# The keys of the last six chunks turned by DMA instead of on TensorE, and most of the instruction order rewritten

## The chip, the cores and the metric

The kernel runs on one core of a Trainium2 chip. The core has a matrix engine (TensorE, PE in the profile, with its weight loads listed as PEld), three engines for elementwise work (VectorE or DVE, ScalarE or ACT, GpSimd or POOL), a sequencer that issues transfers (SyncE or SP), and 16 DMA engines that carry them out. Every engine runs its own instructions strictly in the order in which they were written; engines wait for one another by semaphores. The metric is the device time of one execution in microseconds. Before the change its median over 13 runs was 153.55 us (152.85 to 154.96).

## The reference

The computation is a linear-attention layer followed by a feed-forward layer, on 4 sequences of 768 positions, with 8 heads of 48 channels (384 in all).

```python
for t in range(S):
    cur = np.einsum('bhd,bhe->bhde', u[None] * kt, vt)
    y[:, :, t] = np.einsum('bhd,bhde->bhe', rt, state + cur)
    state = w[None, :, :, None] * state + np.einsum('bhd,bhe->bhde', kt, vt)
...
xn = (x - mu) / np.sqrt(var + 1e-06) * g_ln
ch = np.maximum(xn @ w_ch1, 0.0) @ w_ch2
return x + ch
```

Here `r`, `k`, `v` are [4, 8, 768, 48], `x` is the attention output brought to [4, 768, 384], `w_ch1` is 384 × 1536 and `w_ch2` is 1536 × 384. All inputs and the output are float32; the kernel multiplies in bfloat16.

## The kernel before

The 768 positions of each sequence are cut into 6 chunks of 128 (`NCH`), so there are 24 chunks, numbered 0 to 23 (`NT`). In a chunk the recurrence becomes matrix products. A chunk i passes through these steps, whose names are the words of the written order:

- `k`, `v`, `r` load the inputs on SP's queue (L180, L186); one `r` serves two chunks. Buffers for k and v number 7 each (`LD`).
- `sck` scales the keys by powers of the decay into one of four bfloat16 buffers (L361, on DVE or POOL); `scr` does the same for r, in two halves (L364).
- `TK` turns the scaled keys on PE: four transposes of 128 × 128 into the PSUM bank `tr` (L379). `kT` copies the result to SBUF (L383, on ACT or DVE). `TR` and `rT` do this for r (L394, L400).
- `q` multiplies rT by the turned keys (L411). Chunks from 8 on (`QP`) take the keys straight from PSUM, as long as they are turned on PE (`qp(i)`). `cc` sums q with the bonus weights on PE (L438), `cp` copies that out (L449), `Vb` multiplies it into v (L453, POOL).
- `at` multiplies kT by rT on PE, giving the scores (L418); `A` masks them on DVE (L428).
- `kv` multiplies the keys by the values (L469); `S` adds the state (L484) and `Z` applies the decay (L493 or L497), giving the state for the next chunk. `vc` casts v (L370).
- `y` puts state and scores together on PE (L509, L521), `x` adds the bonus on DVE (L534), `xn` centres (L548, L552), `sq` and `rs` give the variance (L561, L572).
- `lc` turns xn into `xT`: for chunks from 8 on by a DMA transpose on SP (L613), before that on PE (`ln`).
- `up` multiplies by the first weights (L630), `re` is the rectifier (L644 on ACT, L646 on DVE), `dn` multiplies by the second weights (L657), `ot` adds x (L667), `st` stores (L678). `up` and `re` work on groups: chunks 0 to 5 alone, then pairs, so groups 6 to 14 hold chunks 6 and 7 up to 22 and 23; `up12_3` is unit 3 of group 12. `dn18` has three parts.

Which instruction follows which is given by `ORDER` (L23 to L67), a list of these words. A suffix names the engine (`.V` DVE, `.A` ACT, `.G` POOL, `.S` SP) where it differs from the default. `Planner.order` walks the list and emits each step; the costs and due times given to `add` (L762 on) play no part any more, but each step's needs are asserted to stand ahead of it. So the list fixes the sequence of every engine, and also of SP's queue of loads, stores and transposes. PE alternates between attention steps and the large products `up` and `dn`, which fill it up.

`KP` (L590) is the first chunk whose keys are turned by DMA; before the change it is 24, so none is. The branch for it is there (L785: a step `kT` on SP that calls `transpose_k_by_dma`, L385). The step `sckb` (L768) says what has to be done before a scaled-key buffer is written again.

Of the kernel before, what the change touches and what calls it, by code (L numbers as in the profile page):

```python
# [29 lines left out]
up2_2 re2_2.V rT5.A TK4 kT4.A q4.G kv3 Z3 up1_1 re1_1.V at4 A4 vc4.G xn3.A w2l1 ln3 up2_1 lc3.A cc4 cp4.A TK5 sq1  # L30
w2s03.V re2_1.A w2s02.G Vb4 up3_2 kv4 w2s01.V rs0 w2s11.G kT5.A w2s00.A y4 x4 xn4.A w2s13.A w2s10.A w2l2 up3_1
re3_1.A w2s20.G at5 dn00 r3 scr31.G q5.V re3_2.V w2s12.V ln4 lc4.V Z4 up3_0 re3_0.A dn01 cc5 v5 w2s23.A w2s22.A
cp5.A Vb5 A5 up4_2 up4_0 w2s21.V dn02 re4_2.A up4_1 scr30.V TR3 sq4 k6 ot0 sq2 sq3 vc5.V y5 r4 re4_1.V k7 rT7.A
rT6.A dn10 dn11 re4_0.A x5 xn5.V ln5 lc5.V dn12 ot1 sck6.G TK6 scr40.G sck7.V up5_0 up5_1 v6 rs1 kT6.A q6.V TK7
kT7.A scr41.V at6 A6 cc6 cp6.A Vb6 dn20 st0.S TR4 q7.V vc6.A kv6 Z6 re5_1.A k8 rT9.A rT8.A dn21 y6 x6 sck8.G at7
A7 dn22 ot2 xn6.A TK8 cc7 cp7.A v7 up5_2 re5_0.A kT8.A re5_2.A vc7.G kv7 S7 Vb7 k10 k9 sck9.G v8 y7 Z7.G x7 xn7.A
r5 dn30 q8 vc8.A at8 A8 v9 k12 dn31 st1.S r6 scr50.G ln6 lc6.V dn32 ot3 cc8 y8 ln7 sq5 lc7.A kv8 S8 dn40 cp8.A
TK9 kT9.A q9 up6_2 dn41 v10 k11 st2.S v12 v13 sq6 scr51.G up6_1 re6_1.A re6_2.A vc9.V sck10.V cc9 cp9.A TR5 Vb8
x8 dn42 rs2 k13 xn8.V lc8 Z8.G scr61.G ot4 Vb9 scr60.G at9 A9 up6_3 kv9 S9 Z9.G dn50 r7 rT11.A rT10.A TK10 q10
sck11.V re6_3.A kT10.A sq7 dn51 y9 x9 up6_4 re6_4.A sck12.V xn9.A lc9 rs3 vc10.G at10 TK11 cc10 q11 kT11.A cp10.A  # L40
up6_0 re6_0.A dn52 A10 up6_5 re6_5.A TR6 st4.A rT13.A rT12.A vc12.G y10 kv10 Vb10 ot5 dn60 at11 dn61 x10 S10
Z10.G cc11 cp11.A A11 xn10.V sck13.G scr70.G v11 vc11.V k15 TK12 kT12.A st5.A dn62 k14 k18 up7_4 at12 re7_4.A
Vb11 up7_5 q12 ot6 re7_5.A sq8 y11 cc12 cp12.A TK13 scr71.G lc10 r8 sq10 dn70 up7_0 up7_2 A12 kT13.V x11 q13
xn11.A lc11 re7_2.V TR7 y12 rT14.A rT15.A vc13.V at13 kv12 Z12 v14 A13 Vb12 up7_1 re7_1.A re7_0.A sq9 sck14.G
dn71 cc13 TK14 cp13.V kT14.V q14 dn72 kv13 up7_3 re7_3.A x12 ot7 xn12.A sck15.G S13 scr81.G scr80.G up8_4 TK15
kT15.V at14 k16 sq12 A14 dn80 up8_3 y13 rs4 re8_3.A sq11 re8_4.A q15 dn81 at15 k17 TR8 rT16.A r9 st3.S cc14
cp14.A up8_5 rT17.A re8_5.A dn82 up8_1 vc14.G Vb13 Z13.V x13 sck16.V TK16 Vb14 xn13.V A15 up8_0 kv14 v15 vc15.G
v17 lc12 st6.S re8_1.A up8_2 sck17.G ot8 dn90 q16 S14 Z14.V scr91.G sck18.G y14 x14 lc13 kT16.A re8_2.A sq13
scr90.V v16 k20 dn91 at16 cc15 dn92 re8_0.A cp15.V A16 ot9 Vb15 TK17 up9_3 kT17.A v23 st8.S v19 r10 k19 xn14.V
lc14 k21 vc17.G rs5 kv15 up9_1 re9_1.A y15 q17 S15 Z15.G vc16.A re9_3.A dn100 x15 xn15.V lc15 TR9 rT19.A at17  # L50
up9_2 cc16 dn101 v21 A17 re9_2.V cp16.V up9_0 re9_0.A dn102 rT18.V scr101.G Vb16 rs6 kv16 up9_4 ot10 S16 Z16.G
TK18 kT18.A sck19.V dn110 y16 x16 st9.S re9_4.A v18 scr100.G dn111 up9_5 cc17 q18 v22 re9_5.A dn112 at18 sq14 A18
TK19 cp17.A kT19.A up10_5 re10_5.A up10_0 y17 vc18.G r11 Vb17 cc18 cp18.A up10_1 vc19.G ot11 st11.A Vb18 q19
sck20.G st10.S k23 TR10 dn120 re10_0.V up10_4 xn16.V rT21.V lc16 dn121 scr111.G sck21.G vc21.A kv18 dn122 x17 Z18
ot12 st12.S rT20.A re10_1.A at19 A19 TK20 kT20.A cc19 y18 dn130 up10_3 at20 cp19.A re10_4.A xn17.A lc17 q20 TK21
kT21.A x18 dn131 A20 up10_2 q21 re10_2.V dn132 ot13 sq18 scr110.G re10_3.A TR11 rT23.V sq15 Vb19 rs7 sq16 kv19
S19 k22 sck22.V v20 y19 x19 rT22.A dn140 up11_1 sq17 re11_1.A dn141 cc20 st13.A cp20.A TK22 kT22.A dn142 at21
up11_0 up11_4 xn18.A vc22.V sck23.V q22 TK23 ot14 xn19.V lc18 lc19 st14.S A21 Z19.G rs8 vc20.G kv20 Vb20 S20
Z20.G re11_0.A kT23.A y20 up11_5 dn150 re11_4.V at23 x20 xn20.V cc21 q23 A23 cp21.A Vb21 re11_5.A up11_2 kv21
dn151 S21 Z21.V up11_3 re11_3.A re11_2.A y21 dn152 sq19 ot15 st15.S cc22 at22 kv22 S22 Z22.G up12_3 dn160 up12_2  # L60
vc23.G A22 x21 cp22.A re12_3.A cc23 dn161 lc20 y23 xn21.V lc21 cp23.A dn162 up12_4 re12_4.A Vb23 re12_2.V up12_1
re12_1.A Vb22 ot16 dn170 up12_5 x23 y22 xn23.A lc23 x22 re12_5.V xn22.V lc22 rs9 dn171 up12_0 dn172 ot17 sq22
up13_0 st17.S re12_0.A up13_5 re13_5.A st7.A re13_0.V dn180 up13_3 re13_3.V dn181 up14_0 re14_0.A sq20 dn182 ot18
up13_4 re13_4.V up13_2 re13_2.A sq23 dn190 up14_3 dn191 up13_1 st18.A re13_1.V dn192 re14_3.A ot19 st19.A up14_4
re14_4.V up14_5 re14_5.A sq21 rs11 rs10 dn200 up14_1 re14_1.A st16.S dn201 up14_2 re14_2.A dn202 ot20 dn210 dh00
dn220 dh01 dn221 dh02 oh0 dn222 ot22 st20.A dn211 dh10 sh0.A st22.A dn212 ot21 st21.S dh11 dh12 oh1 sh1.S
"""  # L67


class Planner:  # L70
# [12 lines left out]
    def add(self, name, eng, cost, fn, needs=(), takes=(), gives=(), pri=0, load=0.0, kind=None,  # L83
            alt=None, lands=1.9, after=0.0):

        t = dict(name=name, eng=eng, cost=cost, fn=fn, needs=list(needs), takes=list(takes),
                 gives=list(gives), pri=pri, load=load, kind=kind, alt=alt, lands=lands, end=None,
                 first=(eng, cost), after=after)  # L90
# [27 lines left out]
def kernel(  # L118
# [17 lines left out]
    NCH = S // L  # L136
# [106 lines left out]
    NSC, NSR = 4, 2  # L243
# [116 lines left out]
    def scale_k(i, eng):  # L360
        eng.tensor_tensor(out=k_bufs[i % NSC][:, :, :D], in0=k_t[i][:], in1=Fk[:], op=ALU.mult)  # L361
# [10 lines left out]
    def k_bank(i):  # L372
        return "y" if i < 1 else "tr"

    def transposes_k(i):
        sc = k_bufs[i % NSC].rearrange("p (q e) d -> p q (e d)", e=2)
        tk_t[i] = ps.tile([P, 2 * HP, P], BF16, name=k_bank(i))
        for q in range(HP):
            nc.tensor.transpose(out=tk_t[i][:, q, :], in_=sc[:, q, :], identity=ident[:])  # L379
# [9 lines left out]
    def transposes_r(e):  # L389
        sc = r_bufs[e % NSR].rearrange("p j (q e) d -> p j q (e d)", e=2)  # L390
        tp_t[e] = ps.tile([P, 2 * HP, P], BF16, name="tr")
        for j in range(2):
            for q in range(HP):
                nc.tensor.transpose(out=tp_t[e][:, j * HP + q, :], in_=sc[:, j, q, :], identity=ident[:])  # L394
# [192 lines left out]
    LNP = 8  # L587
    LNO = 4
    ln_done = []
    KP = 24  # L590
    SZ, QP = 6, 8
    ot_t = {}

# [124 lines left out]
    add = plan.add  # L718
# [22 lines left out]
    for rank, (a, i) in enumerate(seq):  # L741
        pri = 50 - 0.1 * rank
# [19 lines left out]
    for i in range(NT):  # L762
        c = i % NCH
        g, j = tile_group[i]
        last = c == NCH - 1
        p0 = 60 - 2 * i
        e, half = divmod(i, 2)
        add(f"sckb{i}", "", 0.0, None, ([f"TK{i - NSC}"] + ([f"kv{i - NSC}"] if (i - NSC) % NCH < NCH - 1 else [])) if i >= NSC else [], [("sck", i, 1 if last else 2)], pri=p0)  # L768
        add(f"sck{i}", "DVE", 0.7, lambda e, i=i: scale_k(i, e), [f"k{i}", "Fk", f"sckb{i}"], [], [("k", i)], pri=p0, after=35 + (i - 6) * PACE if i > 6 else 0.0,
            alt=[("POOL", 1.0)])  # L770
        if not half:
            add(f"scrb{e}", "", 0.0, None, [f"TR{e - NSR}"] if e >= NSR else [], [("scr", e, 1)], pri=p0)
            for t in range(2):
# [28 lines left out]
        if not last:  # L802
# [19 lines left out]
            pri=p0 + 2, alt=[("DVE", 0.35)])  # L822
# [78 lines left out]
```

## Time and profile before

| | |
|---|---|
| Median of 13 runs | 153.55 us |
| Time of the profiled execution | 153.56 us |
| Its span | 151.8 us, 4482 instructions |
| Key transposes on PE (L379) | 96 matmuls, 24 chunks of four |
| Copies of turned keys (L383) | 20 on ACT at 586 to 589 ns, 4 on DVE at 415 ns |
| Products q on DVE from PSUM, from SBUF; on POOL | 413, 495; 1,156 ns |
| Scaling of keys (L361) on DVE; on POOL | 11 at 708 ns; 13 at 1,054 ns |
| DMA transposes xT (L613) | 16 |
| Loads of k, v, r: issue to landing, median | 3.9, 4.7, 5.1 us |

The span runs from the first to the last instruction of the program. The profile gives for each engine its busy time; for a group of like instructions the count, the mean duration, and the idle time ahead of them with the instruction that ended it. "L379 PE tr" means the instruction of line 379 that writes the tile `tr`. The slices divide the span into 40 equal parts, and each digit is the busy share in tenths. The view by stretches gives, for a window in microseconds, the busy microseconds and counts of each engine, the granted TensorE clock and the share of DMA. The chain of waits follows the work that ended last back to the start.

### The profile page before, as it was taken

How to read it: one execution, taken by the hardware profiler on the slowest of the kernel's cores; microseconds unless marked ns; L12 is line 12 of the kernel's file. 1: busy time of each engine (PE TensorE's matmuls, PEld its weight loads, DVE VectorE, ACT ScalarE, POOL GpSimd, SP SyncE). 2: the span in 40 equal slices, each digit the busy share in tenths (PEclk: the TensorE clock that was granted, in tenths of full speed). 3: DMA queues.
4: the chain of work that ended last, by engine and by line, in shares of the span. 5: the costliest groups of instructions: out<-in, count | busy, mean ns of one | idle time of the engine just before them, and what ended most of it. 6: DMA issues, size and time to landing. Idle time of an engine off the chain costs nothing.

```text
span 151.8 us, 4482 instructions
## 1 busy us (share of the span) xinstructions
PE 142.8 (94%) x1778; PEld 111.9 (74%) x1778; DVE 119.3 (79%) x246; ACT 89.0 (59%) x198; POOL 90.3 (59%) x122
## 2 busy tenths in 40 slices
PE   5959789999999999999999999999999999999991
PEld 5848569988777777777778777776867787777770
DVE  5978999997789699899997897669899884535132
ACT  3445667699677676766768554645863526172300
POOL 8088799578557898599718749398384180011200
PEclk9995999999999999999999999999999999999999
DMA  4999999999799874596894998961533021511032
GB/s 93 255 206 300 294 307 271 316 280 232 173 235 262 200 158 106 129 234 131 155 251 123 230 213 179 230 167 56 97 91 104 34 70 30 181 52 52 0 109 105
DMA packets 75563, 25.47 MB, mean 168 GB/s; under 512 B 69648, under 2 KB 74390, under 8 KB 75542
## 3 DMA queue, kind: packets, MB, share of 16 engines
q1 hardware_dynamic: 72966, 23.11, 63.9%
q10 hardware_dynamic: 2480, 2.07, 4.0%
q8 instruction: 14, 0.23, 0.7%
q14 instruction: 7, 0.06, 0.1%
q0 software_dynamic: 96, 0.01, 0.0%
HBM read 18.88 MB, written 4.72 MB: 155 GB/s over the span
## 4 chain that ended last, share of the span: by engine, by line
PE 83%; DVE 8%; DMA 3%; issue 2%; ACT 1%; POOL 0%; POOLq 0%; SPq 0%; DVEq 0%
PE hp L630 29%; PE o L657 26%; PE at L418 5%; PE tr L394 4%; PE tr L379 3%; PE o L259 3%; PE y L521 3%; DMA k<-in_k_dram 3%; DVE A L428 3%; PE s L469 2%; PE y L509 2%; PE hp L689 1%; PE hp L657 1%; DVE sc L361 1%; PE s L438 1%
## 5 line engine op out<-in xcount | busy, mean ns | idle before, releaser
L630 PE MATMUL hp<-xT,w_sb 128*128 128x256 bf16 (+1 forms) x540 | 57.5, 251 | 0.3 <-ACT w_sb L343 0.3
L657 PE MATMUL o<-w_sb,hT 128*128 128x384 bf16 x264 | 53.5, 326 | 0.0
L630 PEld LDWEIGHTS <-w_sb 128*128 128x128 bf16 x540 | 42.9, 98 | 7.4 <-ACT w_sb L343 0.4
L644 ACT ACTIVATE hT<-hp 128x512 bf16<-128x512 f32 x54 | 31.9, 598 | 22.0 <-PE hp L630 21.4
L657 PEld LDWEIGHTS <-hT 128*128 128x128 bf16 x276 | 24.5, 97 | 10.5
L428 DVE TENSOR_TENSOR A<-at,mask 128x1024 bf16<-128x1024 f32 x24 | 29.2, 1217 | 2.5 <-PE at L418 2.4
L453 POOL TENSOR_TENSOR Vb<-v,cc 128x384 f32<-128x384 f32 x24 | 20.6, 862 | 11.8 <-ACT cc L449 10.0
L364 POOL TENSOR_TENSOR sc<-r,Fr 128x384 bf16<-128x384 f32 x19 | 19.6, 1039 | 6.9 <-DMA r<-in_r_dram 6.9
L667 DVE SCALAR_TENSOR_TENSOR ot<-o,rs,x 128x384 f32<-128x384 f32 x22 | 13.5, 614 | 8.1 <-PE o L657 6.9
L383 ACT COPY kT<-tr 128x512 bf16<-128x512 bf16 x19 | 11.1, 586 | 12.7 <-PE tr L379 9.7
L400 ACT COPY rT<-tr 128x512 bf16<-128x512 bf16 x20 | 13.9, 745 | 4.4 <-PE tr L394 2.6
L534 DVE SCALAR_TENSOR_TENSOR x<-y,Vb 128x384 f32<-128x384 f32 x24 | 13.2, 550 | 3.8 <-PE y L521 3.8
L646 DVE TENSOR_SCALAR hT<-hp 128x512 bf16<-128x512 f32 x18 | 12.3, 684 | 4.0 <-PE hp L630 3.8
L561 ACT ACTIVATE sq<-x,sum 128x384 bf16<-128x384 f32 x24 | 14.6, 610 | 1.3 <-DVE x L534 1.3
L361 POOL TENSOR_TENSOR sc<-k,Fk 128x384 bf16<-128x384 f32 x13 | 13.7, 1054 | 0.0
L493 POOL TENSOR_TENSOR Z<-S,WLZ 128x384 bf16<-128x384 f32 x9 | 9.0, 1001 | 7.8 <-DVE S L484 7.8
L572 POOL TENSOR_SCALAR rs<-sqs 128x2 f32<-128x2 f32 x12 | 2.6, 214 | 18.5 <-ACT sq L561 17.9
L379 PE MATMUL tr<-ident,sc 128*128 128x128 bf16 x92 | 8.9, 219 | 2.5 <-DVE sc L361 2.2
L418 PE MATMUL at<-rT,kT 48*128 48x128 bf16 x192 | 9.7, 222 | 0.0
L379 PEld LDWEIGHTS <-sc 128*128 128x128 bf16 x96 | 6.4, 97 | 4.3 <-DVE sc L361 2.6
L575 POOL TENSOR_TENSOR rs<-rs,expo 128x2 f32<-128x2 f32 x12 | 8.6, 718 | 1.0
L552 ACT ACTIVATE xn<-x,sum 128x384 bf16<-128x384 f32 x12 | 7.4, 615 | 2.6 <-DVE x L534 2.4
(96 smaller groups left out, 204.7 us busy)
## 6 DMA issues: line engine op xcount, KB each, us to landing
r<-in_r_dram SPq DMA_DIRECT2D x12, 384.0 KB, 5.1
k<-in_k_dram SPq DMA_DIRECT2D x24, 192.0 KB, 3.9
wst<-in_moe_w_ch_dram SPq DMA_DIRECT2D x6, 768.0 KB, 7.5
v<-in_v_dram SPq DMA_DIRECT2D x23, 192.0 KB, 4.7
out_dram<-ot SPq DMA_DIRECT2D x14, 192.0 KB, 2.7
out_dram<-ot ACTq DMA_DIRECT2D x9, 192.0 KB, 2.2
xT<-xn SPq DMA_TRANSPOSE x16, 2.4
v<-in_v_dram ACTq DMA_DIRECT2D x1, 192.0 KB, 3.9
```

What stands on the lines that cost most here:

```text
L361: eng.tensor_tensor(out=k_bufs[i % NSC][:, :, :D], in0=k_t[i][:], in1=Fk[:], op=ALU.mult)
L364: eng.tensor_tensor(out=r_bufs[e % NSR][:, j, :, :D], in0=r_t[e][:, :, j * D : (j + 1) * D], in1=Fr[:, j], op=ALU.mult)
L379: nc.tensor.transpose(out=tk_t[i][:, q, :], in_=sc[:, q, :], identity=ident[:])
L400: (eng.copy if eng is nc.scalar else eng.tensor_copy)(out=rT_t[i][:].rearrange("p q (t j) -> p q j t", j=2), in_=tp_t[e][:, :, c * LH : (c ...
L418: nc.tensor.matmul(out=at_t[i][:, par, p, :], lhsT=kT_t[i][p0 : p0 + D, p, :], rhs=rT_t[i][p0 : p0 + D, p, :], start=True, stop=True,)
L428: nc.vector.tensor_tensor(out=A_t[i][:].rearrange("p e q t -> p (e q) t"), in0=at_t[i][:].rearrange("p e q t -> p (e q) t"), in1=mask[:].u ...
L453: nc.gpsimd.tensor_tensor(out=Vb_t[i][:], in0=vf_t[i][:], in1=cc_t[i][:].unsqueeze(2).to_broadcast([P, H, D]), op=ALU.mult)
L561: nc.scalar.activation(out=sq[:], in_=x_t[i][:], func=ACT.Square, bias=sum_t[i][:], scale=-float(C), accum_out=sq_t[e][:, c : c + 1],)
L630: nc.tensor.matmul(out=hp[:, f * gw : (f + 1) * gw], lhsT=w1_sb[:, n, kc, fb * P : (fb + 1) * P], rhs=xT_t[g][:, kc, :gw], start=(kc == 0) ...
L644: nc.scalar.activation(out=out, in_=src, func=ACT.Relu)
L657: nc.tensor.matmul(out=o_t[i][:, :C], lhsT=hT_t[g][:, fk, j * P : (j + 1) * P], rhs=w2_sb[:, fk, :], start=(fk == 0), stop=(fk == FK - 1),)
L667: nc.vector.scalar_tensor_tensor(out=ot_t[i][:], in0=o_t[i][:, :C], scalar=rs_t[i // 2][:, i % 2 : i % 2 + 1], in1=x_t[i][:], op0=ALU.mult ...
```

## The change

Three things are changed. `KP` goes from 24 to 18, so that the keys of chunks 18 to 23 are turned by DMA: their `TK` and the copies on ACT are gone, and a DMA transpose on SP's queue writes kT from the scaled buffer. With that `qp(i)` no longer holds for these chunks, so their `q` reads kT from SBUF and may run on POOL. `sckb` names `kT` where there is no `TK` any more. And in `ORDER` everything after `scr30` is written anew; the words up to there, the loading phase, stay as they are.

```diff
@@ ORDER @@
...
-cp5.A Vb5 A5 up4_2 up4_0 w2s21.V dn02 re4_2.A up4_1 scr30.V TR3 sq4 k6 ot0 sq2 sq3 vc5.V y5 r4 re4_1.V k7 rT7.A
...
-ot12 st12.S rT20.A re10_1.A at19 A19 TK20 kT20.A cc19 y18 dn130 up10_3 at20 cp19.A re10_4.A xn17.A lc17 q20 TK21
-kT21.A x18 dn131 A20 up10_2 q21 re10_2.V dn132 ot13 sq18 scr110.G re10_3.A TR11 rT23.V sq15 Vb19 rs7 sq16 kv19
-S19 k22 sck22.V v20 y19 x19 rT22.A dn140 up11_1 sq17 re11_1.A dn141 cc20 st13.A cp20.A TK22 kT22.A dn142 at21
-up11_0 up11_4 xn18.A vc22.V sck23.V q22 TK23 ot14 xn19.V lc18 lc19 st14.S A21 Z19.G rs8 vc20.G kv20 Vb20 S20
...
+cp5.A Vb5 A5 up4_2 up4_0 w2s21.V dn02 re4_2.A up4_1 scr30.V sq4 k6 sck6.G TR3 ot0 sq2 r4 k7 scr40.G vc5.V y5 dn10
...
+TK17 re8_0.V st8.S k19 k20 sck18.G Vb14 x14 vc17.G Z14.G cp15.A xn14.A sq12 r10 lc14 kv15 scr91.G kT17.A ot9 S15
+up9_0 at16 v21 y15 re9_0.A dn100 up9_1 cc16 cp16.A re9_1.A dn101 kv16 dn102 Z15.V Vb15 kT18 A16 x15 q17 xn15.A
+lc15 up9_2 re9_2.A ot10 st10.A S16 scr90.G up9_4 re9_4.A at17 A17 Vb16 dn110 scr101.G scr100.V cc17 TR9 rT18.A
+dn111 y16 sq13 up9_3 re9_3.A vc21.V cp17.V r11 dn112 ot11 st7.A up9_5 re9_5.V sck19.G kT19 k23 at18 A18 up10_2
+re10_2.A st11.A x16 rT19.V xn16.A vc23.V sck20.G kT20 q18.G Vb17 rs6 Z16.G dn120 up10_5 dn121 up10_3 re10_3.A
+dn122 TR10 up10_1 y17 v18 re10_5.A up10_4 scr111.V v20 k21 ot12 dn130 st12.A re10_1.A rT21.V x17 xn17.A rT20.V
+vc18.G q19.G cc18 scr110.V cp18.V at19 Vb18 up10_0 re10_0.A kv18 lc16 sq14 k22 lc17 sck21.G kT21 dn131 TR11
+re10_4.V A19 Z18 y18 rT23.A x18 dn132 ot13 cc19 cp19.A Vb19 sq15 at20 A20 q20.V y19 kv19 xn18.A dn140 vc20.A S19
+sq18 x19 sck23.G up11_2 dn141 up11_1 kT23 re11_2.A xn19.A Z19.V st9.A cc20 at21 A21 up11_4 kv20 S20 y20 dn142
+at23 rT22.A re11_4.A up11_0 re11_1.A sck22.G rs7 ot14 q21.G dn150 A23 Z20.V sq16 cp20.A up11_5 cc21 Vb20 x20
+dn151 sq19 sq17 re11_0.A cp21.A rs8 v22 st13.S re11_5.A vc22.A kT22 q22.V lc18 q23.V kv21 S21 lc19 Z21.G dn152
+up11_3 ot15 at22 y21 A22 cc22 st14.A re11_3.A dn160 st15.S cp22.A sq20 Vb21 kv22 Vb22 x21 xn21.A S22 Z22.G dn161
+up12_1 re12_1.V y22 dn162 ot16 lc21 up12_2 re12_2.A up12_0 cc23 re12_0.A xn20.V lc20 cp23.A Vb23 dn170 rs9 x22
...
@@ -587,7 +587,7 @@
-    KP = 24
+    KP = 18
@@ -765,7 +765,7 @@
-        add(f"sckb{i}", "", 0.0, None, ([f"TK{i - NSC}"] + ([f"kv{i - NSC}"] if (i - NSC) % NCH < NCH - 1 else [])) if i >= NSC else [], [("sck", i, 1 if last else 2)], pri=p0)
+        add(f"sckb{i}", "", 0.0, None, ([f"TK{i - NSC}" if i - NSC < KP else f"kT{i - NSC}"] + ([f"kv{i - NSC}"] if (i - NSC) % NCH < NCH - 1 else [])) if i >= NSC else [], [("sck", i, 1 if last else 2)], pri=p0)
```

More of the change, by code (lines that the diff above doesn't have):

```diff
@@ L32 @@
 re3_1.A w2s20.G at5 dn00 r3 scr31.G q5.V re3_2.V w2s12.V ln4 lc4.V Z4 up3_0 re3_0.A dn01 cc5 v5 w2s23.A w2s22.A
-cp5.A Vb5 A5 up4_2 up4_0 w2s21.V dn02 re4_2.A up4_1 scr30.V TR3 sq4 k6 ot0 sq2 sq3 vc5.V y5 r4 re4_1.V k7 rT7.A
-rT6.A dn10 dn11 re4_0.A x5 xn5.V ln5 lc5.V dn12 ot1 sck6.G TK6 scr40.G sck7.V up5_0 up5_1 v6 rs1 kT6.A q6.V TK7
-kT7.A scr41.V at6 A6 cc6 cp6.A Vb6 dn20 st0.S TR4 q7.V vc6.A kv6 Z6 re5_1.A k8 rT9.A rT8.A dn21 y6 x6 sck8.G at7
-A7 dn22 ot2 xn6.A TK8 cc7 cp7.A v7 up5_2 re5_0.A kT8.A re5_2.A vc7.G kv7 S7 Vb7 k10 k9 sck9.G v8 y7 Z7.G x7 xn7.A
@@ L37 @@
[L37 to L51, printed above, removed]
@@ L52 @@
-TK18 kT18.A sck19.V dn110 y16 x16 st9.S re9_4.A v18 scr100.G dn111 up9_5 cc17 q18 v22 re9_5.A dn112 at18 sq14 A18
-TK19 cp17.A kT19.A up10_5 re10_5.A up10_0 y17 vc18.G r11 Vb17 cc18 cp18.A up10_1 vc19.G ot11 st11.A Vb18 q19
-sck20.G st10.S k23 TR10 dn120 re10_0.V up10_4 xn16.V rT21.V lc16 dn121 scr111.G sck21.G vc21.A kv18 dn122 x17 Z18
-ot12 st12.S rT20.A re10_1.A at19 A19 TK20 kT20.A cc19 y18 dn130 up10_3 at20 cp19.A re10_4.A xn17.A lc17 q20 TK21
-kT21.A x18 dn131 A20 up10_2 q21 re10_2.V dn132 ot13 sq18 scr110.G re10_3.A TR11 rT23.V sq15 Vb19 rs7 sq16 kv19
@@ L57 @@
-S19 k22 sck22.V v20 y19 x19 rT22.A dn140 up11_1 sq17 re11_1.A dn141 cc20 st13.A cp20.A TK22 kT22.A dn142 at21
-up11_0 up11_4 xn18.A vc22.V sck23.V q22 TK23 ot14 xn19.V lc18 lc19 st14.S A21 Z19.G rs8 vc20.G kv20 Vb20 S20
-Z20.G re11_0.A kT23.A y20 up11_5 dn150 re11_4.V at23 x20 xn20.V cc21 q23 A23 cp21.A Vb21 re11_5.A up11_2 kv21
-dn151 S21 Z21.V up11_3 re11_3.A re11_2.A y21 dn152 sq19 ot15 st15.S cc22 at22 kv22 S22 Z22.G up12_3 dn160 up12_2
-vc23.G A22 x21 cp22.A re12_3.A cc23 dn161 lc20 y23 xn21.V lc21 cp23.A dn162 up12_4 re12_4.A Vb23 re12_2.V up12_1
@@ L62 @@
[L62 to L66, printed above, removed]
+cp5.A Vb5 A5 up4_2 up4_0 w2s21.V dn02 re4_2.A up4_1 scr30.V sq4 k6 sck6.G TR3 ot0 sq2 r4 k7 scr40.G vc5.V y5 dn10
@@ new lines @@
+dn11 scr41.G rT6.A rT7.A re4_0.V re4_1.A x5 sq5 xn5.V ln5 dn12 lc5.V ot1 sck7.V TK6 up5_0 kT6.A q6.V up5_1 TK7
+kT7.A v6 st0.S k8 at6 cc6 vc6.A cp6.A Vb6 A6 q7.V re5_0.A v7 sq3 rs1 sck8.G dn20 TR4 rT9.A rT8.A kv6 Z6 vc7.A
+dn21 v8 y6 x6 xn6.A k9 at7 A7 cc7 dn22 ot2 up5_2 kv7 TK8 y7 st1.S cp7.A kT8.A vc8.V dn30 Vb7 at8 dn31 S7 Z7.G q8
+ln6 x7 xn7.A v9 rs2 r6 sck9.G lc6.A re5_1.A dn32 r5 A8 cc8 ot3 ln7 y8 lc7.A re5_2.A scr60.G scr51.G kv8 S8 vc9.G
+cp8.A Vb8 dn40 k12 k10 sck10.G TK9 q9 kT9.A up6_1 re6_1.A sq6 dn41 cc9 cp9.A Vb9 Z8.V scr50.V k11 st2.S v10 v16
@@ new lines @@
+at9 A9 dn42 ot4 TR5 rT11.A rT10.A v12 k13 r7 up6_5 kv9 S9 up6_3 dn50 x8 re6_5.A sck11.G xn8.A re6_3.A scr61.G
+Z9.G vc10.G TK10 kT10.V dn51 y9 lc8 q10 at10 x9 xn9.V A10 lc9 cc10 up6_2 TK11 q11 kT11.V sq7 re6_2.A sck13.G
+cp10.A dn52 ot5 up6_0 re6_0.A up6_4 re6_4.A kv10 st4.S y10 TR6 rT12.A rT13.A sck12.V S10 Vb10 x10 xn10.A vc16.G
+rs3 vc12.G Z10.G dn60 at11 A11 dn61 cc11 TK12 q12 sq8 kT12.A dn62 ot6 cp11.A up7_0 scr70.V up7_5 v11 re7_0.A sq10
+cc12 at12 A12 r8 k14 v13 k15 scr71.G vc11.A Vb11 TK13 lc10 kT13.A k16 sq9 q13 dn70 sck14.G kv12 y11 x11 xn11.A
@@ new lines @@
+lc11 dn71 cp12.V re7_5.A Vb12 TR7 rT14.A rT15.A at13 vc13.G up7_3 re7_3.V y12 up7_2 re7_2.A dn72 Z12 x12 A13
+scr80.G TK14 kT14.A q14 up7_4 re7_4.V up7_1 re7_1.V cc13 cp13.A sq11 at14 sck15.G y13 TK15 st5.S ot7 kT15.A kv13
+v14 k17 v19 st6.S q15 xn12.A up8_3 re8_3.A up8_4 re8_4.V sck16.G k18 v15 v23 v17 lc12 Vb13 scr81.G x13 S13 A14
+dn80 TR8 rT16.A rT17.A dn81 xn13.A lc13 up8_2 cc14 cp14.A dn82 rs4 ot8 Z13.V vc14.G TK16 at15 rs5 q16 kT16.V
+up8_1 dn90 kv14 A15 S14 vc19.A dn91 sck17.V re8_2.A st3.A up8_5 re8_1.A r9 up8_0 y14 cc15 dn92 re8_5.A vc15.A
@@ new lines @@
+dn151 sq19 sq17 re11_0.A cp21.A rs8 v22 st13.S re11_5.A vc22.A kT22 q22.V lc18 q23.V kv21 S21 lc19 Z21.G dn152
+up11_3 ot15 at22 y21 A22 cc22 st14.A re11_3.A dn160 st15.S cp22.A sq20 Vb21 kv22 Vb22 x21 xn21.A S22 Z22.G dn161
+up12_1 re12_1.V y22 dn162 ot16 lc21 up12_2 re12_2.A up12_0 cc23 re12_0.A xn20.V lc20 cp23.A Vb23 dn170 rs9 x22
+y23 sq22 xn22.V lc22 x23 xn23.V lc23 up12_4 re12_4.A dn171 up12_5 re12_5.A up12_3 re12_3.A dn172 ot17 up13_5
+up13_0 re13_5.A re13_0.V dn180 up13_3 st16.A re13_3.A sq21 dn181 up14_0 re14_0.V dn182 ot18 st18.S up13_2
@@ L67 @@
+re13_2.V up13_4 dn190 up14_3 re14_3.V re13_4.A dn191 up13_1 re13_1.V dn192 up14_1 up14_5 sq23 re14_1.A ot19 dn200
+st19.S up14_4 re14_4.V re14_5.A dn201 up14_2 re14_2.A dn202 dn210 dh00 rs11 st17.S rs10 ot20 dn220 dh01 dn221
+st20.S dh02 oh0 sh0.S dn222 ot22 st22.A dn211 dh10 dn212 ot21 st21.S dh11 dh12 oh1 sh1.A
 """
```

## The prediction

> **What bounds the kernel now.** I read the page first, for each engine's share and then for where in the span that share falls.
>
> ```profile
> span 151.8 us, 4482 instructions
> PE 142.8 (94%) x1778; PEld 111.9 (74%) x1778; DVE 119.3 (79%) x246; ACT 89.0 (59%) x198; POOL 90.3 (59%) x122
> PE   5959789999999999999999999999999999999991
> DVE  5978999997789699899997897669899884535132
> DMA  4999999999799874596894998961533021511032
> ```
>
> TensorE (PE) is full in every slice from the sixth to the last but one; VectorE (DVE) comes near it in many. As a busy PE may hide pipelined waiting, I then read the busy time by stretches (PE, weight load, DVE, ACT and POOL, then clock, DMA share, GB/s).
>
> ```profile
> 50.00:60.00 10.00, 10.00 (x134) 7.70 (x132) 8.53 (x18) 6.99 (x18) 8.74 (x12) 1.00 0.73 164
> 70.00:80.00 10.00, 9.76 (x132) 7.67 (x132) 9.76 (x21) 7.49 (x16) 5.58 (x8) 1.00 0.80 178
> 90.00:100.00 10.00, 10.00 (x125) 7.92 (x123) 7.59 (x15) 4.79 (x11) 6.26 (x9) 1.00 0.86 198
> 110.00:120.00 10.00, 9.67 (x129) 7.30 (x128) 9.14 (x19) 5.32 (x13) 4.96 (x7) 1.00 0.27 75
> ```
>
> PE falls short of its ten only where DVE is above nine. The clock is 1.00, so no time is to be had there. The view of PE's waits from 37 us on confirms it: two are named, 0.3 and 0.2 us. The first lies in the chain of waits, and is a late key chunk:
>
> ```profile
> 105.72 0.60 ACT kT L383
> 106.43 3.92 DMA k<-in_k_dram
> 110.37 0.57 DVE sc L361
> 110.98 0.40 PE tr L379 x4
> ```
>
> k22 was issued at 106.4, landed 3.9 us later, was scaled, and only then could PE transpose it. So from 37 to 148 us the time is PE's own work in the order written. A change pays by what it takes from PE, and costs what PE then waits for.
>
> **The change part by part.**
>
> *Six transposes leave PE.* The timeline of PE shows what one chunk costs there:
>
> ```profile
> 92.97 0.39 PE L379 MATMUL tr<-ident,sc 128*128 128x128 bf16 x4
> 93.20 0.81 PE L657 MATMUL o<-w_sb,hT 128*128 128x384 bf16 x4
> ```
>
> The 0.39 us overlaps the next work, which starts 0.23 us later; 0.22 to 0.23 is also the spacing after the other five (TK19 to TK23). Six by 0.225 give -1.35 us, all on the path.
>
> *Six evacuations leave ACT* (L383, 586 ns each, 3.5 us). From 90 us on ACT is idle for over three us in ten: worth nothing now. Had they been late, PE's scores would have waited, and no such wait is in PE's view.
>
> *Six products change.* q18 to q23 read kT from SBUF instead of PSUM: 495 ns on DVE for 413, and three go to POOL at 1,156 ns. That is DVE -1.0 us, POOL +3.5 us. They now also wait for the DMA.
>
> *Six DMA transposes enter SP's queue.* The only rows are those of xT; the line L613 over the whole span, then from 110 us on (min/median/max, ns of issue and us to landing):
>
> ```profile
> L613 SPq DMA_TRANSPOSE xT<-xn x16: 1179/1189/2138, 55.2 to 128.6; - x16
> DMA to landing us min/median/max: 2.3/2.4/3.8
> ...
> L613 SPq DMA_TRANSPOSE xT<-xn x6: 1179/1182/1206, 112.5 to 128.6; - x6
> DMA to landing us min/median/max: 2.3/2.3/2.4
> ```
>
> They carry three 128-wide blocks, the keys four. SP is held 1.19 us by one; four thirds of it, an estimate, is 1.6, so 9.5 us for six. SP's timeline has normal issues at about 0.55 us and stretches of many us waiting on stores, so the hold itself has room; what counts is the landing. I measure cushions in PE work between two words of the new order (units from this trace: up 0.655, dn 0.65, at 0.33, cc 0.10, kv 0.17, y 0.37, TR 0.45). From kT18 to at18 there are 5.8 us, then 7.1 (19), 9.4 (20) and 5.6 (21): hidden even at a landing of 3.8. From kT23 to at23 there are 2.3 and from kT22 to at22 only 1.5 (kv21, dn152, up11_3). But SP can issue these two sooner than they are written, as soon as POOL has scaled the keys (1.05 us). sck22 is written 3.5 us of PE work before at22, sck23 4.2 before at23. So scaling plus landing takes 1.05 + 2.4 = 3.45: both in time, with nothing to spare on 22. With the longest landing, 3.8, it takes 4.85: 1.3 and 0.6 short. Bounds: 0 and +1.9 us. A gain from this step is excluded, since no score of 18 to 23 waits now. I take 0.3, near the low end: half of the landings are at 2.4 or below, and the six from 110 us on, where keys 22 and 23 would fall, lie at 2.3 to 2.4.
>
> Behind kT22 on SP stand lc18, lc19 and st15; up12, which needs lc19, is written 3.6 us of PE work after it. Behind q22 on DVE stand q23, S21, ot15 and A22, so a late key 22 also holds DVE, the engine next in line.
>
> *The rest is re-ordered.* Every word after scr30 may move, loads and stores on SP included, scalings and decays between DVE and POOL. From scr30 to the end POOL gets 2.5 us more work and DVE 4.7 us less. Two places can be read. First, k22 is now issued 8.8 us of PE work ahead of its scaling (before: directly ahead). That landing took 3.9, so PE's pause there, 0.46 us around TK22, goes: -0.46. It is late next only if POOL is, which has sck23 ahead of sck22. Second, DVE from scr111 to q23: summed by the rows (A 1.22, S 0.55, x 0.63, Z 0.57, ot 0.61, rT 0.73, scr 0.55), the new order has 17.0 us of it against 12.8 of PE, the old 16.6 against 13.6. The surplus grows from 3.1 to 4.2 us: DVE must run ahead 1.1 us more than before or PE waits. Bounds 0 and +1.1. DVE can run ahead: from 59.5 us of PE work after scr30 (x16, rT19, vc23) to 64.9 the new order gives it 2.0 us only. I take 0.4, nearer the low end for that. For the other moves I take 0: PE's other pauses from 37 us on (0.40 at up7_2, 0.24 of it in the view of waits) may go or be replaced. That is the bound on the gain, -0.64 us more; the loss is bounded by the rivals.
>
> The sum: -1.35 - 0.46 + 0.3 + 0.4 = -1.1 us. The profiled execution took 153.56 us (151.8 of span and 1.8 around it), the median of the runs is 153.55: the same within 0.01, so 153.55 - 1.1 = 152.4 us.
>
> *A rule against the change.* The row first: a chunk on PE costs 0.225 us of PE and 0.586 of ACT, a DMA transpose of three blocks 2.4 us to landing. The Trainium skill (VectorE: DVE Perf Modes, section Rules for kernel authors) says to transpose 128×128 on TensorE where a PSUM result is acceptable and by DMA only otherwise; its table of the three paths puts a block at 390 ns against 1,309. By that table, taken as exposed latency, four blocks cost 3.7 us more, and six chunks 22 us: about 176 us. By the row's spacing PE is relieved of 0.225 a chunk and the latency is covered, which gives 152.4. The trace does not agree with 390 ns as a price on a filled PE: four blocks take 0.225 us of it.
>
> **The rivals.**
>
> *A. DVE takes PE's place.* PE is relieved but DVE's surplus counts in full (+1.1) along with the 0.3 for late keys: 153.55 - 1.35 - 0.46 + 1.1 + 0.3 = 153.1, no measurable change. For: DVE at 9.76 and 9.14 where PE falls short. Against: 4.7 us less DVE work overall.
>
> *B. The keys of 22 and 23 come late (slower).* Place: at22 and at23, written 3.5 and 4.2 us of PE work after their scalings. Price: with a landing of 3.8, 1.9 us; and each us that POOL scales late comes on top for both. In this trace L361 on POOL follows Vb (L453), which waits 10.0 us in all for ACT's cc, so 1 us late is near: 3.9 us together, 153.55 - 1.35 - 0.46 + 3.9 = 155.6. It is slower by over 0.5% once these waits pass 1.81 + 0.77 = 2.6 us. For: no slack on 22, in-order PE, and q22 holding DVE. Against: SP and POOL have idle time there, and the DMA share is down to 0.27.
>
> *C. The new order also loses the other pauses.* No late key, no DVE surplus, and 0.64 us gained: 153.55 - 1.35 - 0.46 - 0.64 = 151.1.
>
> *D. The change removes nothing from the path*, if PE waits as long in those six places as it worked there: 153.55 - 0.46 + 0.3 + 0.4 = 153.8. For: its order is fixed. Against: PE has filler (up, dn) all the way to the end.
>
> **How the numbers follow.** Forecast 0.44, A 0.14, B 0.24, C 0.10, D 0.08. A difference of 0.5%, 0.77 us, is about what a measurement of this kernel can tell from no change. Faster by more: the forecast except where its costs run to their middle (0.38), and C: 0.48. Within: A, D and the rest of the forecast, less 0.01 to rounding: 0.27. Slower: B, and a hundredth: 0.25. The range reaches down to C's 151.1 and up to 155.2, most of B. The likeliest case's own range is 151.7 (no late key, no surplus) to 153.0.
>
> **What would show it.** Right: L379 on PE falls from 96 matmuls to 72; sixteen plus six DMA transposes on SP, landing in 2.3 to 3.8 us; no PE wait named at L418 for a kT over 0.3 us; no key DMA in the chain around TK22's old place; PE at 9.7 or more of ten in every stretch from 37 to 140 us; a span near 150.7. Wrong: PE or its weight load waiting at L418 on DMA kT around scores 22 and 23; DVE above 9.5 of ten with PE below between scr111 and q23; SP held at L387 with the xT transposes behind it late, so that L630 waits for xT; or pauses of PE at places that the old order did not have.

## The result and the profile after

The changed kernel takes 151.80 us (median of 11 runs, 151.15 to 154.58), against 153.52 us for the kernel before (48 runs). The ratio is 0.9897, with a 95% interval of 0.9871 to 0.9923: 1.6 us faster, between 1.2 and 2.0 (it leaves out executions that were slower than the rest, here the one of 154.58). The forecast was 152.4, faster by 1.1.

The page of the changed kernel, for the share of the engines:

```profile
span 149.9 us, 4440 instructions
PE 141.1 (94%) x1754; PEld 111.0 (74%) x1754; DVE 118.2 (79%) x237; ACT 89.6 (60%) x200; POOL 94.0 (63%) x123
```

PE's busy time fell by 1.7 us and its share stayed at 94%: it still sets the time. The groups of PE show the transposes that are left, 72 instead of 96 (the four into `y` are chunk 0):

```profile
L379 PE MATMUL tr<-ident,sc 128*128 128x128 bf16 x68 | 6.6, 219 | 1.7 <-DVE sc L361 1.0 <-ACT rT L400 0.7
...
L379 PE MATMUL y<-ident,sc 128*128 128x128 bf16 x4 | 0.4, 219 | 0.0
```

The view by stretches, for three of the stretches shown of before (same columns; the fourth, 50 to 60 us, has PE at 9.96):

```profile
70.00:80.00 10.00, 10.00 (x128) 8.15 (x126) 7.96 (x15) 7.63 (x17) 8.17 (x12) 1.00 0.81 180
...
90.00:100.00 10.00, 10.00 (x106) 7.47 (x105) 8.19 (x14) 4.70 (x10) 7.47 (x9) 1.00 1.13 195
...
110.00:120.00 10.00, 10.00 (x129) 7.39 (x128) 8.58 (x16) 7.36 (x20) 6.84 (x9) 1.00 0.54 143
```

The two stretches in which PE had fallen short, 9.76 and 9.67, are full now. But PE falls short in a stretch that was full before, the one from 37 us on (the first line is the kernel before, the second the changed one):

```profile
37.00:50.00 13.00, 13.00 (x189) 9.91 (x187) 11.62 (x24) 10.09 (x22) 8.60 (x11) 1.00 0.99 219
37.00:50.00 13.00, 12.37 (x178) 9.21 (x176) 11.53 (x23) 8.60 (x20) 7.49 (x10) 1.00 0.99 217
```

The new DMA transposes are the line L387:

```profile
L387 SPq DMA_TRANSPOSE kT<-sc x6: 1189/1206/1286, 89.5 to 111.3; - x6
DMA to landing us min/median/max: 2.4/3.7/5.0
```

They hold SP 1.2 us each, as those of three blocks do, but land later than those: 3.7 us in the median and up to 5.0, against 2.4 and 4.6 (of the six landings the profile has five; that of key 22 is missing). And these are all waits that the view of PE names from 37 us on:

```profile
PE tr L605 <- ACT sq L561: 0.4, 1, 0.4
PE y L521 <- DVE vv L370: 0.2, 1, 0.2
```

No wait at L418: no score waited for a key. Both lines are new. The first stands at 40.0 us, where the new order lets PE reach the transposes of chunk 5's xn before that is ready (the row names sq, which ends with xn). The second stands at 38.0 us, at y5, which waits for its cast v. Measured by the time from one instruction of PE to the next, against what the same pair takes elsewhere, PE lost 0.55 us at the one place and 0.41 at the other.

The two spans differ by 1.9 us, but not all of it is the change's. Both kernels run the same instructions up to the transposes TR3. These are the rows of TR3 and of PE's last group of matmuls, before and after:

```profile
37.47 0.61 PE L394 MATMUL tr<-ident,sc 128*128 128x128 bf16 x8
147.65 0.82 PE L689 MATMUL hp<-w_sb,hT 128*128 128x192 bf16 x8
```

```profile
36.92 0.61 PE L394 MATMUL tr<-ident,sc 128*128 128x128 bf16 x8
145.58 0.82 PE L689 MATMUL hp<-w_sb,hT 128*128 128x192 bf16 x8
```

TR3 began 0.55 us earlier after the change. The 0.55 us are chance: over the fourteen profiles of this document, which all have the same instructions up to there, TR3 began between 36.40 and 37.67 us. From TR3 to PE's last group it was 110.18 us before and is 108.66: 1.52 less, which agrees with the runs. The same measure of pauses shows where it comes from. PE's pauses of over 0.1 us from TR3 on add up to 1.2 us before (0.46 at TK22, 0.40 at TR7, 0.19 and 0.12) and to 1.2 us after (0.55 and 0.41 as above, and 0.20). So the pauses only changed places, and what is left is the work of the six transposes.

### The profile page after: what moved, and what is told of

The parts are those of the page before. It is cut to its first block, busy times and chain, and to the rows that moved or that the text cites. A ratio compares the mean times of both kernels' runs of the same rounds, so it can differ in the third digit from the quotient of the medians.

```text
span 149.9 us, 4440 instructions
## 1 busy us (share of the span) xinstructions
PE 141.1 (94%) x1754; PEld 111.0 (74%) x1754; DVE 118.2 (79%) x237; ACT 89.6 (60%) x200; POOL 94.0 (63%) x123
## 4 chain that ended last, share of the span: by engine, by line
PE 88%; DVE 5%; ACT 2%; issue 2%; POOL 0%; POOLq 0%; DVEq 0%
PE hp L630 32%; PE o L657 28%; PE at L418 5%; PE tr L394 3%; PE o L259 3%; PE y L521 3%; PE tr L379 2%; PE y L509 2%; PE s L469 2%; DVE A L428 2%; PE hp L689 1%; PE s L438 1%; PE hp L657 1%; PE hp L300 1%; ACT rT L400 1%
## 5 line engine op out<-in xcount | busy, mean ns | idle before, releaser
L630 PE MATMUL hp<-xT,w_sb 128*128 128x256 bf16 (+1 forms) x540 | 57.0, 251 | 0.3 <-ACT w_sb L343 0.3
L630 PEld LDWEIGHTS <-w_sb 128*128 128x128 bf16 x540 | 43.0, 98 | 7.6 <-ACT w_sb L343 0.4
L644 ACT ACTIVATE hT<-hp 128x512 bf16<-128x512 f32 x52 | 30.8, 597 | 24.2 <-PE hp L630 23.7
L453 POOL TENSOR_TENSOR Vb<-v,cc 128x384 f32<-128x384 f32 x24 | 21.3, 889 | 11.7 <-ACT cc L449 9.8
L361 POOL TENSOR_TENSOR sc<-k,Fk 128x384 bf16<-128x384 f32 x18 | 18.8, 1050 | 3.7 <-PE s L469 3.2
L364 POOL TENSOR_TENSOR sc<-r,Fr 128x384 bf16<-128x384 f32 x16 | 16.2, 1023 | 6.5 <-DMA r<-in_r_dram 6.5
L646 DVE TENSOR_SCALAR hT<-hp 128x512 bf16<-128x512 f32 x20 | 13.6, 685 | 8.5 <-PE hp L630 8.4
L552 ACT ACTIVATE xn<-x,sum 128x384 bf16<-128x384 f32 x18 | 11.1, 617 | 6.2 <-DVE x L534 5.8
L383 ACT COPY kT<-tr 128x512 bf16<-128x512 bf16 x13 | 7.6, 584 | 6.2 <-PE tr L379 5.4
L418 PE MATMUL at<-rT,kT 48*128 48x128 bf16 x192 | 9.5, 219 | 0.0
L521 PE MATMUL y<-vv,A 128*128 128x48 bf16 x192 | 8.7, 183 | 0.2 <-DVE vv L370 0.2
L259 PE MATMUL o<-ident 128*128 128x128 bf16 x67 | 7.1, 263 | 1.6 <-DVE ident L234 1.6
L411 POOL TENSOR_TENSOR q<-rT,kT 128x512 bf16<-128x512 bf16 x6 | 7.1, 1176 | 2.4 <-ACT kT L383 2.4
```

The lines of the kernel that those rows point to most:

```text
L364: eng.tensor_tensor(out=r_bufs[e % NSR][:, j, :, :D], in0=r_t[e][:, :, j * D : (j + 1) * D], in1=Fr[:, j], op=ALU.mult)
L418: nc.tensor.matmul(out=at_t[i][:, par, p, :], lhsT=kT_t[i][p0 : p0 + D, p, :], rhs=rT_t[i][p0 : p0 + D, p, :], start=True, stop=True,)
L453: nc.gpsimd.tensor_tensor(out=Vb_t[i][:], in0=vf_t[i][:], in1=cc_t[i][:].unsqueeze(2).to_broadcast([P, H, D]), op=ALU.mult)
L630: nc.tensor.matmul(out=hp[:, f * gw : (f + 1) * gw], lhsT=w1_sb[:, n, kc, fb * P : (fb + 1) * P], rhs=xT_t[g][:, kc, :gw], start=(kc == 0) ...
L644: nc.scalar.activation(out=out, in_=src, func=ACT.Relu)
L646: nc.vector.tensor_scalar(out=out, in0=src, scalar1=0.0, scalar2=None, op0=ALU.max)
```

## Experiments: is it PE's work, or the order?

Theory P says that the gain is the work taken off PE. Rival O says that the rewritten order brings it. The first experiment gives PE its work back and leaves all else:

```diff
 at_t[i] = ps.tile([P, 2, HP, P], FP32, name="at")
+for p in range(HP if i >= KP else 0):
+    nc.tensor.matmul(out=at_t[i][:, 0, p, :], lhsT=ident[:], rhs=ident[:], start=True, stop=True)
```

> The changed kernel with four extra matmuls of 128 columns ahead of the scores of each of chunks 18 to 23, on operands that are always there; the scores overwrite what they wrote. So PE gets back the work that the six key transposes took (6 x 0.225 = 1.35 us) and nothing else is undone. Theory P (the gain is PE's own work): the whole 1.35 us comes back, 151.8 + 1.35 = 153.15 us, a ratio to the kernel before of 0.998. Rival O (the gain is the rewritten order, whatever PE does): PE has slack, 151.8 us, ratio 0.989.

Measured: 153.05 us, ratio 0.9976 (0.9952 to 0.9999). Against 0.9897 that is 0.79% of 153.5, 1.2 us (0.7 to 1.7 with both intervals combined), where 1.35 was expected. The traces say it more sharply. These are the scores of chunk 8 in the changed kernel, whose last group of PE began at 145.58 us as shown above, and then both rows in this one (its lines count two more):

```profile
48.63 0.40 PE L418 MATMUL at<-rT,kT 48*128 48x128 bf16 x8
```

```profile
47.44 0.40 PE L420 MATMUL at<-rT,kT 48*128 48x128 bf16 x8
145.80 0.82 PE L691 MATMUL hp<-w_sb,hT 128*128 128x192 bf16 x8
```

Between them lie 96.95 and 98.36 us: 1.41 more. P holds: from there on a microsecond of PE work is a microsecond of time. (From TR3 the traces differ by 0.74 only, because the pauses at 38 and 40 us were short in this execution.)

The next two give each part alone. First the DMA steps in the old order, at the places of TK:

```diff
-TK18 kT18.A sck19.V dn110
+kT18 sck19.V dn110
(and so for 19 to 23; KP = 18)
```

> The old order with keys 18 to 23 turned by DMA: each TK word becomes the DMA step, its copy on ACT is left out. Theory P with the cushions: PE loses 1.35 us of work, but in the old order only 1.6 us of PE work stand between the word of key 20 and its scores and 1.7 us for key 23, against a landing of 2.4 to 3.8 us: each is 0.7 to 2.2 us short. 153.5 - 1.35 + 1.4 to 4.4 = 153.6 to 156.6 us, with PE waiting at L418 for kT. A rival by which the landing is hidden in any order gives 152.2; rival O gives 153.5 with no wait at L418.

Measured: 161.45 us, ratio 1.053 (1.050 to 1.057), outside what either theory gave. The view of waits, over all engines and then PE from 40 us on, says why:

```profile
DVE q L411 <- DMA kT<-sc: 9.7, 5, 3.1
...
PE hp L630 <- DVE hT L646: 2.7, 2, 2.3
PE at L418 <- DMA kT<-sc: 1.8, 2, 1.1
```

The scores waited only 1.8 us. The products q, left where a key in PSUM had been ready at once, stopped DVE for 9.7 us, and with it what is queued behind them on DVE, rectifiers among it (hence PE waiting at L630).

Then the new order with the keys turned on PE:

```diff
-Vb15 kT18 A16
+Vb15 TK18 kT18.A A16
-re10_3.A dn122 TR10
+re10_3.A TK20 kT20.A dn122 TR10
...
-    KP = 18
+    KP, KQ = 24, 18   # qp(i) and TR's need ask for KQ
```

> The new order with keys 18 to 23 turned on PE again and copied out by ACT; the products q still read from SBUF and stand where they stood. The transposes stand near the places of the DMA steps, moved where the one PSUM bank of the transposes is taken (19 behind rT19, 20 ahead of TR10, 21 ahead of TR11 behind dn132, rT22 earlier for 23). Theory P: 1.35 us more PE work than the changed kernel, 153.1 us, up to 0.4 more for the shared bank; ratio 0.997 to 1.0. Rival O: 151.8 us, ratio 0.989.

Measured: 158.96 us, ratio 1.027 (1.022 to 1.032). It doesn't decide between the theories: PE waited 1.9 us at one transpose for the one PSUM bank, as rT19 is copied out late by DVE in this order. So I gave the bank back sooner (the edit is shown against the changed kernel; TK19 now stands behind A18):

```diff
-TR9 rT18.A dn111 ... x16 rT19.V xn16.A
+TR9 rT18.A rT19.A dn111 ... x16 xn16.A
-dn121 up10_3 re10_3.A dn122 TR10
+dn121 TK20 kT20.A up10_3 re10_3.A dn122 TR10
```

> The new order with keys 18 to 23 on PE and ACT again, as in the first attempt (158.9 us, where PE lost 1.9 us at TK19 to the one PSUM bank, held until rT19 was copied, and 1.0 to copies of kT), but with rT19 copied by ACT right behind rT18, and TK20 and TK21 one unit of PE work ahead of TR10 and TR11. The products stay where they were, from SBUF. Theory P (the gain is the 1.35 us of PE work): 153.1 us, up to 153.8 where the bank still makes PE wait. Rival O (the order alone brings the gain): 151.8 us.

Measured: 154.90 us, ratio 1.010 (1.006 to 1.014). Beside it the changed kernel was run again:

> The changed kernel itself, beside the other three on one chip, so that they can be compared with it directly: 151.8 us, ratio 0.989.

Measured: 152.21 us, ratio 0.9896 (0.9853 to 0.9939). So the new order without the DMA steps is 2.0% slower than with them, about 3.1 us: the 1.35 us of PE work, and pauses that the transposes on PE bring along (0.8 us for a rectifier that stood behind a copy of turned keys on ACT, 0.3 at TK21 for its scaled key, both named in its view of PE's waits). These make 2.45; the rest is not accounted for. O falls, in the two placings tried: neither half gives the gain. The new order is slower without the DMA steps, and the old order is slower with them.

The second profile of the changed kernel differs from the first. From TR3 to PE's last group it took 109.03 us instead of 108.66, and PE's waits from 37 us on were:

```profile
PE s L469 <- DVE cc L449: 0.3, 1, 0.3
PE tr L605 <- DVE xn L548: 0.3, 1, 0.3
PE at L418 <- DMA kT<-sc: 0.2, 1, 0.2
```

The last is key 21: it landed at 110.25 us and its scores began at 110.30. So key 21 sits at the edge, and in this execution it was late.

Would moving those few words have been enough? In the old order I put each DMA step behind its scaling and each product shortly ahead of its cc:

```diff
-sck18.G y14 ... cc17 q18 v22 ... up10_5 re10_5.A
+sck18.G kT18 y14 ... cc17 v22 ... q18 up10_5 re10_5.A
(and so for 19 to 23; KP = 18)
```

> The old order with keys 18 to 23 by DMA again, but with the twelve words that matter moved: each DMA step right behind its scaling, each product q shortly ahead of its cc. In the old order with the words left where TK stood, the kernel took 161.4 us: DVE waited 9.7 us at q for landings. Theory Q (what the rewritten order is needed for is the place of these twelve words on SP and DVE): most of the 8 us goes, 152.2 to 153.8 us. Rival O (the whole order has to be rewritten for it): 156 us or more.

Measured: 165.02 us, ratio 1.072 (1.068 to 1.076). Theory Q in this form falls. A step placed early on SP stands there until its key is scaled, and the queue behind it stands too: in the profiled execution (166.88 us, the longest of its six) SP's own waits at the DMA steps were 5.6 us, 3.9, and 3.3 in two, and PE waited 3.9 us at its products `up` for xT transposes that came late. Which places in the order are needed beyond these was not settled.

## Experiments: the prediction's two costs

The prediction put +0.4 us on DVE's surplus of work and +0.3 on late keys. For the first, three products go from POOL to DVE:

```diff
-q18.G  q19.G  q21.G
+q18.V  q19.V  q21.V
```

> The changed kernel with q18, q19 and q21 on DVE instead of POOL: 3 x 0.495 = 1.5 us more for DVE between 93 and 112 us, 3.5 less for POOL. The prediction's rival A (DVE's surplus of work over PE counts in full): 151.8 + 1.5 = 153.3 us, and PE below ten in that stretch. Theory now (DVE runs ahead of PE there, so the surplus costs nothing until the lead is used up): 151.8 to 152.3 us. As DVE's in-order queue would then also wait for key 21, which landed at 109.6 with its product at 111.1, a wait of DVE on the landing of under 1 us may appear.

Measured: 152.03 us, ratio 0.9901 (0.9864 to 0.9938). There is no cost. From 88 to 125 us the products from SBUF now took DVE 2.7 us (six at 458 ns) instead of 1.5 (three at 540), so 1.2 us were added rather than 1.5. DVE's busy time in the three stretches (third number of each) rose from 8.19, 9.28 and 8.58 to:

```profile
90.00:100.00 10.00, 10.00 (x107) 7.51 (x105) 8.76 (x16) 4.73 (x10) 6.83 (x9) 1.00 1.04 184
100.00:110.00 10.00, 10.00 (x133) 7.94 (x132) 9.35 (x19) 7.03 (x16) 5.22 (x6) 1.00 0.69 153
110.00:120.00 10.00, 10.00 (x129) 7.39 (x127) 8.79 (x19) 7.23 (x20) 6.15 (x9) 1.00 0.55 146
```

and PE stayed at ten of ten. From the scores of chunk 8 to PE's last group it took 96.96 us, against 96.95 in the changed kernel. For the second, key 22 is issued later:

```diff
-kT22 q22.V lc18 q23.V kv21 S21 lc19 Z21.G dn152
+lc18 q23.V kv21 S21 lc19 Z21.G kT22 q22.V dn152
```

> The changed kernel with the DMA step of key 22 behind the two xT transposes 18 and 19 on SP (and q22 behind Z21), so that it is issued about 3.9 us later: at about 115.2 instead of 111.3, landing at 117.6 to 119 against scores at 117.0. Theory P with rival B's price (each us that a key lands late is a us of PE): +0.6 to +2.0 us, 152.4 to 153.8, with PE waiting at L418 for kT. If PE's filler or the queue hides it: 151.8. The prediction said that key 22 had nothing to spare: then the whole 3.9 us would show, 155.7.

Measured: 152.75 us, ratio 0.9924 (0.9890 to 0.9957), not apart from 0.9896. The step was issued at 114.8 us instead of 111.3, landed at 117.3, and the scores began at 117.9. As this execution runs 0.9 us later up to there (scores 22 began at 117.0 in the changed kernel), the step moved by 2.6 us against its scores, from 5.7 us ahead of them to 3.1, and still landed 0.6 ahead. PE's waits name no key. So key 22 had some 3.2 us to spare, where the prediction said none.

## Experiments: the pause around k22, and going further

The term of 0.46 us for k22 can be had alone, in the old order:

```diff
-kv19 S19 k22 sck22.V
+kv19 S19 sck22.V
-kv18 dn122
+kv18 k22 dn122
```

> The kernel before with one word moved: k22 is issued behind kv18 instead of directly ahead of its scaling, about 4 us sooner. The prediction's term (PE's pause of 0.46 us around TK22 is the landing of k22): 153.5 - 0.46 = 153.0 us, and neither k22 in the chain of waits nor PE waiting at L379 there. Rival: the pause only moves (sck22 is on DVE behind S19 and its four-buffer wait), 153.5 us.

Measured: 153.24 us, ratio 0.997 (0.994 to 1.000), which fits 0.46 us but hardly stands out. Its trace shows the pause gone. Another of 0.64 us stands at TR10, where PE waits for a product of DVE; but that is at 99.8 us, and k22 is issued at 102.2, so the moved word did not bring it. From TR10 (99.37 us before, 99.76 here) to PE's last group (147.65, 147.57) it took 48.28 us before and 47.81 here: 0.47 less. So the one pair of traces shows the term at its size, and the runs do not contradict it.

If PE work is the price, more chunks by DMA should gain more:

```diff
-    KP = 18
+    KP = 16
-TK16 at15 rs5 q16 kT16.V ... cc15 dn92 ... TK17 ... kT17.A
+kT16 at15 rs5 ... cc15 q16 dn92 ... kT17 ...
```

> The changed kernel with two more chunks, 16 and 17, turned by DMA (KP 16, the DMA steps at the places of TK16 and TK17, q16 moved behind cc15). Theory P: another 2 x 0.225 = 0.45 us off PE, and 6 us of PE work stand between either step and its scores: 151.35 us, ratio 0.987. Rival: DMA is already 0.94 to 1.13 busy from 80 to 100 us, so that the two transposes land late or make the loads late: 152 us or more, with PE waiting at L418 or L379.

Measured: 154.12 us, ratio 1.0044 (1.0017 to 1.0071): 2.3 us slower than with 18, where P gave 0.45 faster. SP's queue in that run, from the timeline:

```profile
75.83 4.04 SPq L185 DMA_DIRECT2D v<-in_v_dram  x3
79.97 2.71 SPq L612 DMA_TRANSPOSE xT<-xn  x2
82.78 1.22 SPq L386 DMA_TRANSPOSE kT<-sc  x1
```

Key 16 had been scaled at 73.8 us and stood behind three loads and two transposes until 82.8. It landed at 85.6, just ahead of its scores at 86.0, so the scores did not wait. DVE did, at the product q16, and then PE at y15 for a step of DVE behind that product:

```profile
DVE q L410 <- DMA kT<-sc: 2.4, 1, 2.4
```

```profile
PE y L508 <- DVE x L533: 0.8, 1, 0.8
```

The profiled execution, 152.73 us, was the fastest of its twelve, so it can't show all of the 2.3 us. The place of key 16 on SP was moved:

```diff
-sck16.G k18 v15 v23 v17 lc12
+sck16.G kT16 k18 v15 v23 v17 lc12
```

> As the kernel with KP 16, but the DMA step of key 16 stands on SP right behind its scaling, ahead of k18 and the loads v15, v23, v17, instead of behind two xT transposes: in that run the key had been scaled at 73.8 us, was issued at 82.8 and landed at 85.6, and PE lost 1.0 us at its scores and 0.45 at kv15. Theory Q (SP's in-order queue, not PE or DMA bandwidth, made those two chunks dear): PE's pause at the scores of 16 goes, 154.1 - 1.5 = 152.6 us or less, down to 151.35. Rival (16 DMA engines are full there, so any extra transfer delays the loads): 154 us again, with PE waiting elsewhere.

Measured: 152.93 us, ratio 0.9934 (0.9904 to 0.9964): 1.1% better from one word moved on SP, so its place in the queue was the dear part. But not better than the changed kernel. The key now landed 7 us ahead of its scores, and PE's longest wait became one for what stands behind it on SP:

```profile
PE hp L629 <- DMA xT<-xn: 0.8, 1, 0.8
...
PE at L417 <- DMA kT<-sc: 0.3, 1, 0.3
```

(Lines are one less in this kernel: L629 is `up`, L417 the scores. The scores that waited are again those of key 21.) One chunk more instead of two:

```diff
-    KP = 18
+    KP = 17
-TK17 re8_0.V ... kT17.A
+kT17 re8_0.V ...
```

> The changed kernel with one more chunk, 17, by DMA, at the place of TK17 (with KP 16 it landed 2.2 us ahead of its scores at worst). Theory P: -0.22 us against the changed kernel, 151.6 us if it is at 151.8. Rival (SP's queue has no room left between 83 and 93 us, and an xT transpose or a load behind it comes late): 152.2 us or more.

Measured: 152.71 us, ratio 0.9935 (0.9903 to 0.9966), against 0.9896 (0.9853 to 0.9939) for the changed kernel run beside it. No gain; the intervals overlap, so a loss isn't shown either. No version beat the changed kernel.

## Why the prediction was right, and where its sizes were off

- **Six transposes off PE, -1.35.** Right. Giving PE the same work back cost 1.2 us by the runs and 1.41 by the traces, and rival D is gone with that.
- **k22's pause, -0.46.** Right: the pause is gone in the changed kernel. Alone, in the old order, its trace is 0.47 us shorter from TR10 on; the runs gave 0.3%, with an interval that reaches to no change.
- **Late keys, +0.3.** Mis-sized: it measured 0 in one profile of the changed kernel and 0.2 in the other, and there at key 21, not at 22 or 23. The step that failed is "with nothing to spare on 22". I counted the cushion from the written place of the scaling, 3.5 us ahead of the scores, but POOL and SP ran ahead of it: the key was scaled 7.2 us and its step issued 5.7 us before its scores, and 2.6 us later still did. The tight one was key 21, which I had called hidden. I counted 5.6 us from its DMA step and left out the 1.05 us of scaling that stands at the same place; the step was issued 4.5 us before its scores, and the landing took 4.1 (109.6 us for scores at 110.1). My upper bound for a landing, 3.8, was passed by the 5.0 of key 20, and by the 6.0 of key 19 in the second profile.
- **DVE's surplus, +0.4.** Mis-sized: it measured 0, and 1.2 us more on DVE didn't show. Rival A had no ground; DVE running ahead, the cover that I named, was enough. But DVE's 4.7 us less work, named against A, were only 1.1 on the page (119.3 to 118.2): like instructions took longer in the new order (scaling r 665 ns for 551, Z by L493 833 for 597, q from SBUF 554 for 495). Why is open.
- **All other moves, 0.** Mis-sized: +0.4. The pause of 0.40 at up7_2 (it stands at TR7, behind up7_2) went, but one of 0.55 ahead of chunk 5's transposes came, and the one at y5 grew from 0.12 to 0.41. Pauses at new places were among the signs that I had named for being wrong, and so was PE below 9.7 of ten: from 37 to 50 us it was 12.37 of 13.
- **The sum.** -1.35 - 0.46 with +0.44 for these moves and none of the two costs is -1.37. Measured from TR3 to PE's last group: -1.52, and -1.15 in the second profile; by the runs: -1.6. The mechanism is the predicted one, but that the sum lies near is in part luck: costs of 0.7 us that I had named did not come, and 0.4 us that I had not named did. Of rival C's further gain nothing was left.
- **Rival B (keys late).** Not in this order. In the old order it came at more than its price: the scores lost 1.8 us, DVE 9.7 at the products. The prediction had named q22 holding DVE, but priced only the scores.
- **The rule against the change.** The Trainium skill (VectorE: DVE Perf Modes, section Rules for kernel authors) says to transpose 128×128 on TensorE where a PSUM result will do. In this kernel that loses: with nearly the same order, keys on TensorE give a ratio of 1.010 and keys by DMA 0.9896. PE's time is what is short here, and the landing of a transpose, 2.4 to 6.0 us in the two profiles of the changed kernel, is nearly all covered.

## What to carry to other kernels

On an engine that is full, price a step by the time to the next instruction's start, and check the price by giving the work back. Where a step moves to a DMA queue, look first at the in-order engine whose instruction waits for the landing (here DVE's product, not PE's scores), and then at what stands behind the step on the issuing queue. Moving the step and its consumers alone was not enough in the old order. Count cushions from where queues really run in a trace, not from written places.

## What was not expected of the hardware

- A DMA transpose of four 128-wide blocks held SP for 1.21 us in the median of the changed kernel (1.19 to 1.29), no longer than one of three (1.20 there, 1.19 before, with single ones up to 2.1); I had estimated 1.6. In other runs single ones of four took up to 2.9.
- Its landing ranged from 2.4 to 5.0 us, to 6.0 in the second profile of the same kernel, and to 6.1 in the runs with two chunks more and with the late key. The longest, key 20 in the changed kernel (5.0) and key 19 with two chunks more (6.1), were issued right behind and ahead of loads of r, k and v on the same queue; from 90 to 100 us DMA was 1.13 busy in the changed kernel. That the loads are the cause is not shown.
- PE's granted clock in the loading phase differed between executions of the same instructions (0.69 and 1.00 from 10 to 15 us). The time to TR3 doesn't simply follow it: in the run with the late key the clock was 1.00 from 10 to 25 us, and TR3 began at 37.47 us as in the kernel before. With TR3 anywhere from 36.40 to 37.67 us, a single pair of spans can mislead by over a microsecond here.
